# Two rows per partition, one 128-wide turn, and a last product formed transposed: three edits to the expert stage of a fused attention, soft-MoE and MLP kernel

## The chip, the cores and the metric

The kernel runs on one core of a Trainium2 chip. The time is that of one execution on the device, in microseconds (us). It was run three times: 636.4, 634.4 and 634.56 us, median 634.56 us. A fourth execution was recorded by the profiler; its own time is 633.09 us, of which the instructions span 631.3 us.

## What is computed

Three layers follow each other, on 4608 tokens of width 512:

```python
# 1 attention through 32 packed vectors, 8 batches x 8 heads, 576 rows each
p_packed = softmax(scale * p @ k.T) @ v
x = softmax(scale * q @ p_packed.T) @ p_packed      # rearranged to (4608, 512)
# 2 soft mixture of 8 experts, 4 slots each: 32 slots in all
logits = x @ phi                                    # (4608, 32)
slot_input = softmax(logits, over tokens).T @ x     # (32, 512)
for e in range(8):                                  # w1: 512x1024, w2: 1024x512
    slot_out[e] = relu(slot_input[e] @ w1[e]) @ w2[e]
y = softmax(logits, over slots) @ slot_out          # combine weights (4608, 32)
# 3 an MLP with h * tanh(softplus(h)), w_in: 512x2048, w_out: 2048x512, both float64 in memory
h = y @ w_in ; out = mish(h) @ w_out
```

The kernel never forms `y`: it multiplies the 32 rows of `slot_out` with `w_in` once (32x2048) and applies the combine weights to that product.

## The kernel before

The work is in three stages. The attention (up to about 162 us of the span) goes batch by batch. The expert stage (162 to about 217 us) reads the weights of the eight experts, 4 MB each, and forms `slot_out`. The MLP (to the end) goes through 18 blocks of 256 tokens and four groups of 512 hidden features; its products use fp32r operands in a high and a low part, and some of its blocks use a seven-product scheme (lines 1316 to 1367).

**Loads.** All weights come on the queue of SyncE (SP). The list `jobs` fixes their order: first and second weights of experts 0 to 5 in turn, with pieces of `w_in` between, then the first weights of experts 6 and 7, the second weights of 6 and 7, then `w_out`. Each job is a chunk of 512 KB. `plan` gives each job a place in large buffers (AW, AC, AY and others); `pump` issues the next job when the former user of its place is done. A first weight's chunk has 128 rows of 4 KB, one per partition (line 146). A second weight's chunk has 256 rows of 2 KB: partition p holds rows p and p+128 of the chunk, in two pieces (line 156). The very last chunk (expert 7, number 3) is read as two loads of half the size (line 154).

**One expert.** `ex_h(e)` multiplies the 32 slot inputs with `w1[e]` (line 989) and copies the hidden row block to SBUF (line 996). `ex_x(e)` picks the expert's four slots with the selection matrix `idm` and, with a VectorE transpose and a relu, leaves `h1T`: hidden features on partitions, 32 slots wide, eight blocks (lines 1004 to 1009). `ex_o(e)` multiplies each block with its rows of `w2[e]` (line 1016): `h1T` is the stationary operand of 32 columns, the weights are the moving one of 512 columns, and four blocks run side by side in four column strips of TensorE, each adding into its strip of the PSUM tile `so`. Rows of `so` other than the expert's four stay unchanged, since `idm` is zero there.

**Combine weights.** `combine(c)`, for batches 4c to 4c+3, is a generator of three parts: the softmax over slots, its normalisation, and the split in a high part `Hm`, `Hr` (fp32r) and a low part `Lm`, `Lr` (lines 1056, 1057). `combine_t(L, b)` turns one batch with TensorE, so that the tile CS holds high, low, high, low in strips of 32 partitions: 4 strips times 5 column blocks, 20 fp32 matmuls with 32-column weights (line 1068), then two copies to CS (line 1074).

**The end of the stage.** After `ex_o(7)`, VectorE copies the left half of `so` to SBUF (line 1419) and ScalarE the right half (line 1420); TensorE transposes the four quarters while summing the four strips with `ids` (line 1425); VectorE copies the result to SOT (line 1429). SOT times `w_in` (`emit_mp`, line 1141) opens the MLP; its second products are those of line 1327. `fill` is a filler matmul that nobody reads. The conversions of `w_out` (`cvt`) stand between on ScalarE and VectorE.

Each engine runs its instructions in the order in which they are written; a manual schedule fixes that order. In the profile one fp32 matmul counts as two weight loads and two passes, an fp32r one as one of each.

Of the kernel before, what the change touches and what calls it, by code (L numbers as in the profile page):

```python
# [19 lines left out]
def kernel(  # L20
# [24 lines left out]
    FT1 = F1 // 128  # L45
# [102 lines left out]

    def job_w2(e, c):
        def emit(t):  # L150
            if (e, c) == (E - 1, 3):
                for f in range(2):
                    r = 256 * c + 128 * f
                    nc.sync.dma_start(out=t[:, DM * f:DM * f + DM], in_=w2[e, r:r + 128, :])
                return
            nc.sync.dma_start(
                out=t[:, 0:2 * DM].rearrange("p (f n) -> p f n", f=2),
                in_=w2[e, 256 * c:256 * c + 256, :].rearrange("(f p) n -> p f n", p=128),
            )
        return emit  # L160

# [84 lines left out]
    ident = const.tile([128, 128], F32, name="ident")  # L246
# [10 lines left out]
    ids = const.tile([128, 32], F32, name="ids")  # L257
# [11 lines left out]
    si_acc = one.tile([128, HQ * D], F32, name="si_acc")  # L269
    st = {b: {} for b in range(B)}  # L270

    held = []

    def cv_z(nm, i, fold=True):

        if nm == "wi":
            name, dst = (nm, i // 4, i % 4), win[i // 2][:, 512 * (i % 2):512 * (i % 2) + 512]
        else:
            name = (nm, i)
            if 4 <= i < 8:  # L280
                if i % 2 == 0:
                    held.append(ring_a.tile([128, 18 * D], F32, tag=f"ring{i // 2 - 2}", name="held"))
                dst = held[i // 2 - 2][:, 512 * (i % 2):512 * (i % 2) + 512]
            else:
                dst = t2.tile([128, 512], F32, name="w64", tag="w64", bufs=4)
        tv = take(*name)[:, 0:1024].bitcast(I32).rearrange("p (n z) -> p n z", z=2)
        if fold:
            nc.scalar.activation(out=dst, in_=tv[:, :, 1].bitcast(F32), func=AF.Prelu, scale=2.0 ** -112, alpha=-(2.0 ** 32))
        else:
            nc.scalar.activation(out=dst, in_=tv[:, :, 1].bitcast(F32), func=AF.Copy, scale=2.0 ** -112)  # L290
        return nm, i, name, dst, dst.bitcast(I32), tv, fold
# [535 lines left out]
    x, y = B - 2, B - 1  # L827
# [143 lines left out]
    ex = {}  # L971
# [26 lines left out]

    def ex_x(e):

        h1 = ex[e][0].rearrange("p (k c j) -> p k c j", c=4, j=32)
        xp = ps_x.tile([128, FT1, M], F32, name="xp", tag="x")
        for c in range(4):
            nc.tensor.matmul(
                xp[32 * c:32 * c + 32], lhsT=idm[:, M * e:M * e + M], rhs=h1[:, :, c], start=True, stop=True,
            )
        h1T = two.tile([128, FT1, M], F32, name="h1T", tag="h1T")
        nc.vector.transpose(out=h1T.rearrange("p k m -> p (k m)"), in_=xp.rearrange("p k m -> p (k m)"))
        nc.vector.tensor_scalar_max(out=h1T, in0=h1T, scalar1=0.0)
        ex[e][1] = h1T  # L1010

    def ex_o(e, n=FT1, w=0, lo=0):
        h1T = ex[e][1]
        for ft in range(lo, n):
            g = ft % 4
            nc.tensor.matmul(
                so[32 * g:32 * g + 32], lhsT=h1T[:, ft], rhs=take("w2", e, ft // 2)[:, (ft % 2) * DM:(ft % 2 + 1) * DM],
                start=(e == 0 and ft < 4), stop=(e == E - 1 and ft >= n - 4),
            )
            if ft % 2:  # L1020
                done("w2", e, ft // 2)
                if ft < n - 1:
                    warm(w)

    def combine(c):

        if c:
            Lm, Hm = (two.tile([128, 512], F32, name=x, tag=x, bufs=1) for x in ("Lm", "Hm"))
        else:
            Lm, Hm = (t2.tile([128, 512], F32, name=x, tag="w64", bufs=4) for x in ("Lm", "Hm"))  # L1030
        Lm, Hm = (x.rearrange("p (b i m) -> p b i m", b=4, i=4) for x in (Lm, Hm.bitcast(F32R)))
        Lr = two.tile([64, 4, M], F32, name="Lr", tag="Lr")
        Hr = two.tile([64, 4, M], F32R, name="Hr", tag="Hr")
        both = ((128, 16, Lm.rearrange("p b i m -> p (b i) m"), Hm.rearrange("p b i m -> p (b i) m")), (64, 4, Lr, Hr))
        for n, k4, L, hi in both:
            lp = ps_x.tile([128, 4, 128], F32, name="clp", tag="x")
            for b in range(4):
                if n == 128:
                    nc.tensor.transpose(lp[:, b], LT[:, 4 * c + b, 0:128], ident)
                else:  # L1040
                    nc.tensor.transpose(lp[0:64, 0, M * b:M * b + M], LT[0:32, 4 * c + b, 128:192], ident[0:32, 0:32])
            xp = lp.rearrange("p b (i m) -> p (b i) m", m=M)[0:n, 0:k4]
            mx = two.tile([128, 16], F32, name="mxc", tag="mxc")
            nc.vector.reduce_max(out=mx[0:n, 0:k4], in_=xp, axis=AX.X)
            nc.vector.tensor_tensor(out=L, in0=xp, in1=mx[0:n, 0:k4, None].to_broadcast([n, k4, M]), op=ALU.subtract)
            nc.scalar.activation(out=L, in_=L, func=AF.Exp)
        yield
        for n, k4, L, hi in both:
            sm = two.tile([128, 16], F32, name="smc", tag="smc")[0:n, 0:k4]
            nc.vector.reduce_sum(out=sm, in_=L, axis=AX.X)  # L1050
            nc.vector.tensor_scalar_add(out=sm, in0=sm, scalar1=1e-9)
            nc.vector.reciprocal(out=sm, in_=sm)
            nc.gpsimd.tensor_tensor(out=L, in0=L, in1=sm[:, :, None].to_broadcast([n, k4, M]), op=ALU.mult)
        yield
        for n, k4, L, hi in both:
            nc.scalar.copy(out=hi, in_=L)
            nc.gpsimd.tensor_tensor(out=L, in0=L, in1=hi.bitcast(F32), op=ALU.subtract)
        Lc[c] = (Hm.bitcast(F32), Hr.bitcast(F32)), (Lm, Lr)
        yield

    def combine_t(L, b):

        cp = ps_h.tile([128, 2, 512], F32, name="cp", tag="hp")
        for i in range(NB):
            n = 128 if i < 4 else 64
            for g in range(4):
                src = L[g % 2][0][:, b % 4, i] if i < 4 else L[g % 2][1][:, b % 4]
                nc.tensor.matmul(
                    cp[32 * g:32 * g + 32, i // 4, (i % 4) * 128:(i % 4) * 128 + n], lhsT=src,
                    rhs=ident[0:n, 0:n] if i < 4 else ident[0:n, 0:n].rearrange("p (j r) -> p r j", j=2),  # L1070
                    start=True, stop=True,
                )
        for src, dst in ((cp[:, 0], CS[:, 512 * b:512 * b + 512]), (cp[:, 1, 0:64], CS[:, TB * 128 + 64 * b:TB * 128 + 64 * b + 64])):
            (nc.scalar.copy if b > 2 else nc.vector.tensor_copy)(out=dst, in_=src)

# [26 lines left out]
    ex_x(4)  # L1102
    next(cb)
    ex_o(4)
    next(cb)
    CS = arena.tile([128, NT], F32R, name="CS", tag="AC")
    combine_t(Lc[0], 0)
    combine_t(Lc[0], 1)
# [14 lines left out]
    ex_x(7)  # L1123
    ex_o(6)
    combine_t(Lc[1], 7)
    ex_o(7)
    late_w = {}
    so_sb = [two.tile([128, DM // 2], F32, name="so_sb", tag="h1") for _ in range(2)]
    SOT = t2.tile([128, 4, M], F32, name="SOT", bufs=1)
# [289 lines left out]
    nc.vector.tensor_copy(out=so_sb[0], in_=so[:, 0:256])  # L1419
    nc.scalar.copy(out=so_sb[1], in_=so[:, 256:512])  # L1420
    ba, bb = bank("x"), bank("x")
    fill(ba)
    cvt("z0 u0")
    for kt in range(4):
        nc.tensor.matmul(
            sot_ps[:, kt], lhsT=so_sb[kt // 2][:, 128 * (kt % 2):128 * (kt % 2) + 128], rhs=ids, start=True, stop=True,
        )
    fill(bb)
    nc.vector.tensor_copy(out=SOT, in_=sot_ps)
    ep.close()  # L1430
# [135 lines left out]
```

## Time and profile before

| | busy us | share of the span |
|---|---|---|
| TensorE matmuls (PE) | 603.5 | 96% |
| TensorE weight loads (PEld) | 522.3 | 83% |
| VectorE (DVE) | 499.5 | 79% |
| ScalarE (ACT) | 339.4 | 54% |
| GpSimd (POOL) | 47.3 | 7% |
| profiled execution | 633.09 whole | span 631.3 |

Busy TensorE time counts overlapping passes once and is no sign of its peak. The share of the 16 DMA engines is at nine tenths or more from about 110 to 221 us and low after that, so the expert stage and the MLP have different limits. HBM read 79.23 MB, written 9.44 MB. The clock row of the page shows nine tenths or more in all its 40 slices.

### The profile page before, as it was taken

What the parts mean: (1) busy time and instruction counts of PE and PEld (TensorE: products, weight loads), DVE (VectorE), ACT (ScalarE), POOL (GpSimd) and SP (SyncE); (2) the same over time, 40 slices, a digit from 0 to 9 for tenths busy, and PEclk for the clock granted to TensorE, in tenths of its full rate; (3) what the DMA queues carried; (4) which work ended last, traced back from release to release, by engine and by line L of the source; (5) the groups of instructions that cost most, each with busy time, mean ns of one, the idle gap of its engine ahead of it and who ended that gap; (6) DMA issues with size and microseconds to landing.
All of it is one profiled execution on the core that took longest, in us unless ns stands there. A gap on an engine that the chain in (4) does not pass through costs nothing.

```text
span 631.3 us, 14397 instructions
## 1 busy us (share of the span) xinstructions
PE 603.5 (96%) x5874; PEld 522.3 (83%) x5874; DVE 499.5 (79%) x1004; ACT 339.4 (54%) x684; POOL 47.3 (7%) x73
## 2 busy tenths in 40 slices
PE   7799999998998999999999999999999999999997
PEld 4577777786434468888989999999999999999997
DVE  4998888978464388988999887788778877887883
ACT  3354555546334486665556555555555555555551
POOL 5122222112030000000000000000000000000000
PEclk9999999999999999999999999999999999999999
DMA  8998963999999962002110110011011101110100
GB/s 274 329 323 293 330 210 128 404 412 407 394 410 413 413 243 67 2 0 68 35 35 0 35 35 12 24 34 34 2 34 34 34 2 34 34 34 2 34 34 35
DMA packets 42162, 89.61 MB, mean 142 GB/s; under 512 B 10736, under 2 KB 19056, under 8 KB 42096
## 3 DMA queue, kind: packets, MB, share of 16 engines
q1 hardware_dynamic: 41696, 88.36, 39.2%
q8 instruction: 46, 0.75, 0.5%
q10 hardware_dynamic: 144, 0.26, 0.1%
q14 instruction: 20, 0.16, 0.1%
q0 software_dynamic: 256, 0.07, 0.1%
HBM read 79.23 MB, written 9.44 MB: 140 GB/s over the span
## 4 chain that ended last, share of the span: by engine, by line
PE 65%; DVE 19%; DMA 8%; ACT 5%; issue 2%; SPq 1%; DVEq 0%; POOL 0%; ACTq 0%; POOLq 0%
PE o L1327 44%; PE so L1327 7%; DMA AW<-in_moe_w_dram 6%; PE h L1205 5%; DVE kT L338 4%; DVE S L1221 2%; DVE A L510 1%; DVE AY L1376 1%; DVE mx L509 1%; PE s L490 1%; DVE Sl L1240 1%; DVE sm L525 1%; DMA AW<-in_q_dram 1%; DVE nmx L386 1%; DMA AC<-in_k_dram 1%
## 5 line engine op out<-in xcount | busy, mean ns | idle before, releaser
L1327 PE MATMUL o<-W,gh 128*128 128x256 f32 (+1 forms) x648 | 119.2, 311 | 0.5 <-DVE AY L1376 0.5
L1327 PE MATMUL o<-T,Sh 128*128 128x256 f32 x708 | 114.8, 284 | 1.0 <-DVE AY L1376 0.9
L1236 ACT CAST gh<-AY 128x512 fp32r<-128x512 f32 x118 | 54.7, 511 | 113.5 <-PE o L1327 113.5
L1327 PEld LDWEIGHTS o<-W,gh 128*128 128x128 f32 x648 | 95.6, 188 | 7.9 <-issue 1.3
L1327 PEld LDWEIGHTS o<-T,Sh 128*128 128x128 f32 x708 | 97.0, 189 | 2.1 <-issue 0.6
L1210 ACT ACTIVATE AY<-h 128x512 f32<-128x512 f32 x126 | 74.0, 594 | 26.3 <-PE h L1205 25.0
L1239 DVE TENSOR_TENSOR gl<-AY,gh 128x512 fp32r<-128x512 f32 x118 | 60.4, 553 | 33.3 <-ACT gh L1236 33.3
L1240 DVE TENSOR_TENSOR Sl<-S,Sh 128x1024 fp32r<-128x1024 f32 x59 | 72.1, 1223 | 9.2 <-ACT Sh L1237 9.2
L1327 PE MATMUL o<-T,Sl 128*128 128x256 f32 x354 | 71.2, 282 | 0.0
L1327 PE MATMUL o<-W,gl 128*128 128x256 f32 (+1 forms) x324 | 70.0, 308 | 0.0
L1237 ACT CAST Sh<-S 128x1024 fp32r<-128x1024 f32 x59 | 61.9, 1049 | 6.8 <-DVE S L1221 6.8
L1205 PE MATMUL h<-CS,W 128*128 128x256 f32 x288 | 56.2, 284 | 0.0
L1327 PEld LDWEIGHTS o<-W,gl 128*128 128x128 f32 x324 | 52.1, 188 | 4.0
L1327 PEld LDWEIGHTS o<-T,Sl 128*128 128x128 f32 x354 | 54.8, 190 | 0.0
L1221 DVE TENSOR_TENSOR S<-AY 128x256 f32<-128x256 f32 x118 | 49.6, 420 | 6.0 <-ACT AY L1210 6.0
L1376 DVE TENSOR_TENSOR AY<-AY,o 128x256 f32<-128x256 f32 x115 | 45.1, 417 | 9.1 <-PE o L1327 5.3
L1205 PEld LDWEIGHTS h<-CS,W 128*128 128x128 f32 x288 | 44.1, 188 | 3.1 <-ACT s L1210 0.8
L1327 PE MATMUL so<-W,gh 128*128 128x256 f32 (+1 forms) x268 | 45.4, 292 | 0.0
L1327 PEld LDWEIGHTS so<-W,gh 128*128 128x128 f32 x268 | 37.3, 188 | 2.4 <-ACT W L1191 0.3
L376 PE MATMUL s<-kT,win 128*128 128x288 f32 x128 | 34.7, 414 | 4.7 <-ACT win L388 3.8
L1327 PE MATMUL o<-W,Sh 128*128 128x256 f32 x236 | 37.5, 281 | 0.0
L490 PE MATMUL s<-win,qT 128*128 128x128 f32 x256 | 32.1, 278 | 1.8 <-ACT win L356 1.8
(263 smaller groups left out, 988.9 us busy)
## 6 DMA issues: line engine op xcount, KB each, us to landing
AW<-in_moe_w_dram SPq DMA_DIRECT2D x45, 512.0 KB, 10.1
r_wo<-in_moe_w_out_dram SPq DMA_DIRECT2D x16, 512.0 KB, 8.9
out_dram<-AY SPq DMA_DIRECT2D x64, 128.0 KB, 2.1
r_wi<-in_moe_w_in_dram SPq DMA_DIRECT2D x13, 512.0 KB, 10.5
AW<-in_q_dram SPq DMA_DIRECT2D x11, 576.0 KB, 5.3
AW<-in_k_dram SPq DMA_DIRECT2D x9, 576.0 KB, 7.3
AW<-in_v_dram SPq DMA_DIRECT2D x40, 128.0 KB, 5.0
AC<-in_moe_w_dram SPq DMA_DIRECT2D x10, 512.0 KB, 10.0
```

The source lines that it names most:

```text
L338: nc.vector.transpose(out=T[:, dh, main].rearrange("p (i r a) -> p a i r" if nm == "k" else "p (i a r) -> p a i r", i=4, a=4,), in_=x[:, 0 ...
L376: nc.tensor.matmul(ps[:, n, 0:288], lhsT=pBD[b % 2][:, hq, dh], rhs=kT[:, dh, 288 * n:288 * n + 288], start=(dh == 0), stop=(dh == 1),)
L490: nc.tensor.matmul(ps[:, k - lo], lhsT=d["qT", hq][:, dh, 64 + 128 * i:192 + 128 * i], rhs=ppBD[b % 2][:, hq, dh], start=(dh == 0), stop=( ...
L1205: nc.tensor.matmul(hp[:, 256 * f:256 * f + 256], lhsT=MS[:, 128 * ft:128 * ft + 128], rhs=CS[:, 256 * n:256 * n + 256], start=True, stop=True,
L1210: nc.scalar.activation(out=s, in_=hp.rearrange("p (f n) -> p f n", f=2), func=AF.Mish)
L1221: nc.vector.tensor_tensor(out=S[:, k], in0=x, in1=y, op=op)
L1236: nc.scalar.copy(out=gh[:, f, t], in_=s[:, f, t])
L1237: nc.scalar.copy(out=Sh, in_=S)
L1239: nc.vector.tensor_tensor(out=gl[:, f, t], in0=s[:, f, t], in1=gh[:, f, t].bitcast(F32), op=ALU.subtract)
L1240: nc.vector.tensor_tensor(out=Sl, in0=S, in1=Sh.bitcast(F32), op=ALU.subtract)
L1327: nc.tensor.matmul(o, lhsT=lhsT, rhs=rhs, start=first, stop=stop)
L1376: add = lambda o, x, y: nc.vector.tensor_tensor(out=o, in0=x, in1=y, op=ALU.add)
```

## The change

1. *Second weights.* A chunk of `w2` is read so that partition p holds rows 2p and 2p+1, one piece of 4 KB. The last chunk is one load as well. `ex_x` picks its columns in the matching order, so its moving operand steps by two elements.
2. *Combine weights.* The split writes high, low, high, low side by side (each part twice, by a repeated read), in tiles `HL` and `HLr`. `combine_t` turns a column block with one fp32r matmul of 128 weight columns instead of four of 32; it reads an fp32r identity that GpSimd makes once. The buffers of 512 columns under the name `w64`, four of them, become two of 1024, shared by `HL` and converted `w_out` pairs. The third part of `combine(1)` moves behind the fourth `combine_t`.
3. *Expert 7.* `ex_o(7)` is dropped. `so` is complete after expert 6 and is copied and transposed into `sot_ps` while the last weights arrive; then 32 matmuls with the weights as stationary operand (128 columns) and `h1T` as the moving one (32 columns) add expert 7 there. One filler goes.

```diff
@@ job_w2
+                out=t[:, 0:2 * DM], in_=w2[e, 256 * c:256 * c + 256, :].rearrange("(p f) n -> p (f n)", f=2),
@@ ex_x
-        h1 = ex[e][0].rearrange("p (k c j) -> p k c j", c=4, j=32)
+        h1 = ex[e][0].rearrange("p (k c j f) -> p k f c j", c=4, j=32, f=2)
...
-                xp[32 * c:32 * c + 32], lhsT=idm[:, M * e:M * e + M], rhs=h1[:, :, c], start=True, stop=True,
+                xp[32 * c:32 * c + 32], lhsT=idm[:, M * e:M * e + M], rhs=h1[:, :, :, c], start=True, stop=True,
@@ combine, third part
-        for n, k4, L, hi in both:
-            nc.scalar.copy(out=hi, in_=L)
-            nc.gpsimd.tensor_tensor(out=L, in0=L, in1=hi.bitcast(F32), op=ALU.subtract)
+        T3 = [t2.tile([128, 1024], F32R, name="HL", tag="w64", bufs=2) for _ in range(2)]
+        T3.append(two.tile([64, 16 * M], F32R, name="HLr", bufs=1))
+        T3 = [t.rearrange("p (k g m) -> p k g m", g=4, m=M) for t in T3]
...
+            r = lambda x: x[:, :, None, :].to_broadcast([n, x.shape[1], 2, M])
+            nc.scalar.copy(out=t[:, :, 0:4:2], in_=r(L))
+            nc.gpsimd.tensor_tensor(out=t[:, :, 1:4:2], in0=r(L), in1=t[:, :, 0:4:2].bitcast(F32), op=ALU.subtract)
@@ combine_t
-            for g in range(4):
-                src = L[g % 2][0][:, b % 4, i] if i < 4 else L[g % 2][1][:, b % 4]
-                nc.tensor.matmul(
-                    cp[32 * g:32 * g + 32, i // 4, (i % 4) * 128:(i % 4) * 128 + n], lhsT=src,
...
+            n, src = (128, L[b % 4 // 2][:, 4 * (b % 2) + i]) if i < 4 else (64, L[2][:, b % 4])
+            nc.tensor.matmul(
+                cp[:, i // 4, (i % 4) * 128:(i % 4) * 128 + n], lhsT=src.rearrange("p g m -> p (g m)"),
+                rhs=ident_r if i < 4 else ident_r[0:n, 0:n].rearrange("p (j r) -> p r j", j=2),
@@ order of the expert stage
-    next(cb)
     CS = arena.tile([128, NT], F32R, name="CS", tag="AC")
...
     combine_t(Lc[0], 3)
+    next(cb)
     ex_x(5)
...
     combine_t(Lc[1], 7)
-    ex_o(7)
@@ end of the stage
-    fill(ba)
     cvt("z0 u0")
+    nc.tensor.matmul(sot_ps, lhsT=ident, rhs=idm[:, None, SPE:SPE + M].to_broadcast([128, 4, M]), start=True, stop=False)
     for kt in range(4):
         nc.tensor.matmul(
-            sot_ps[:, kt], lhsT=so_sb[kt // 2][:, 128 * (kt % 2):128 * (kt % 2) + 128], rhs=ids, start=True, stop=True,
+            sot_ps[:, kt], lhsT=so_sb[kt // 2][:, 128 * (kt % 2):128 * (kt % 2) + 128], rhs=ids, start=False, stop=False,
         )
+    for ft in range(FT1):
+        for kt in range(4):
+            r = DM * (ft % 2) + 128 * kt
+            nc.tensor.matmul(
+                sot_ps[:, kt], lhsT=take("w2", E - 1, ft // 2)[:, r:r + 128], rhs=ex[E - 1][1][:, ft], start=False,
+                stop=(ft == FT1 - 1 and kt == 3),
+            )
```

TensorE's order at the end of the expert stage, before: `xp` and `so` with x8 are experts 7 and 6, `cp` is the last batch's turn, and the second `so` row is expert 7; `o` is a filler and then SOT times `w_in`.

```order
L1004 MATMUL xp<-h_2838,idm 32x256 x4
L1016 MATMUL so<-AW,h1T 32x512 x8
L1068 MATMUL cp<-ident,Hm 32x128
L1068 MATMUL cp<-ident,Lm 32x128
...
L1016 MATMUL so<-AW,h1T 32x512 x8
L1417 MATMUL o_2936<-win_90,ident 128x256
L1425 MATMUL sot_ps<-ids,so_sb 128x32 x4
L1417 MATMUL o_2937<-win_90,ident 128x256
L1141 MATMUL o_2936<-win_90,SOT 32x256 x2
```

The same place after the change (lines are those of the new file); `sot_ps<-h1T,AW` is the new product of expert 7.

```order
L999 MATMUL xp<-h_2755,idm 32x256 x4
L1011 MATMUL so<-AW,h1T 32x512 x8
L1064 MATMUL cp<-ident_r,HL 128x128 x4
L1064 MATMUL cp<-ident_r,HLr 128x64
L1418 MATMUL sot_ps<-idm,ident 128x128
L1420 MATMUL sot_ps<-ids,so_sb 128x32 x4
L1426 MATMUL sot_ps<-h1T,AW 128x32 x32
L1412 MATMUL o_2816<-win_90,ident 128x256
L1136 MATMUL o_2815<-win_90,SOT 32x256 x2
```

The transposition of `so` now stands ahead of expert 7, and eight wide matmuls of it have become 32 narrow ones behind the transposition.

ScalarE's order in the middle of the stage, after the change: the casts of `HL` are the third part of `combine(1)`; before, one cast each of `Hm` and `Hr` stood ahead of the copy of `h` for expert 5, where nothing stands now.

```order
L1036 ACTIVATE Lm<-Lm 128x512
L1036 ACTIVATE Lr<-Lr 64x128
L991 COPY h_2646<-hp 128x1024
L283 ACTIVATE AY<-r_wi_2_2138 128x512
L283 ACTIVATE AY<-r_wi_3_2140 128x512
L1070 CAST CS<-cp 128x512
L1070 CAST CS<-cp 128x64
L1052 CAST HL<-Lm 128x16x32 x2
L1052 CAST HLr<-Lr 64x8x32
L991 COPY h_2718<-hp 128x1024
```

The split for batches 4 to 7 so comes after the turn of batch 3 and shortly before that of batch 4.

## Rows read from the trace of the kernel before

**Rows 1.** Windows: us, busy us (instructions) per engine, granted clock, DMA share, GB/s.

```profile
192.00:195.00 3.00, 1.59 (x44) 0.80 (x36) 2.72 (x7) 1.51 (x4) 0.00 (x0) 1.00 1.03 414
111.00:214.50 103.50, 95.28 (x1340) 57.78 (x1338) 67.02 (x158) 46.56 (x114) 13.97 (x17) 1.00 1.03 407
...
226.00:631.00 405.00, 399.49 (x3073) 382.58 (x3071) 332.90 (x641) 230.04 (x396) 0.85 (x1) 1.00 0.11 32
```

**Rows 2.** Chain that ended last, 185 to 260 us: start, us, what.

```profile
202.48 10.78 DMA AW<-in_moe_w_dram
...
213.30 2.29 PE so L1016 x8
...
217.71 0.61 PE o L1141 x8
...
225.63 1.16 PE so L1327 x4
...
236.44 0.47 PE h L1205 x4
```

**Rows 3.** Waits: PEld from 160 to 232 us, then PE from 225 us on.

```profile
PEld so L1016 <- DMA AW<-in_moe_w_dram: 4.6, 8, 1.4
...
PE o L1327 <- DVE AY L1376: 1.4, 4, 0.4
```

**Rows 4.** Windows while first weights, then second weights, of experts 6 and 7 land.

```profile
194.90:203.60 8.70, 8.48 (x126) 4.07 (x126) 2.00 (x6) 3.47 (x7) 0.00 (x0) 1.00 1.03 413
203.60:213.90 10.30, 9.51 (x126) 4.17 (x126) 3.34 (x9) 3.47 (x7) 0.00 (x0) 1.00 1.05 409
```

**Rows 5.** Groups by form, 162 to 226 us: count, busy us, mean ns.

```profile
L1068 PE MATMUL cp<-ident,Lm 128*32 128x128 f32 x128 | 10.6, 274 | 0.0
...
L1057 POOL TENSOR_TENSOR Lm<-Lm,Hm 128x512 f32<-128x512 f32 x2 | 2.6, 1280 | 0.4 <-ACT Hm L1056 0.4
...
L1425 PE MATMUL sot_ps<-ids,so_sb 128*128 128x32 f32 x8 | 1.1, 280 | 0.0
```

**Rows 6.** Timeline of ACT, then of PEld, around batch 4's turn.

```profile
193.09 0.70 ACT L1074 CAST CS<-cp 128x512 fp32r<-128x512 f32 x2 [0.28 <-PE cp L1068]
...
198.70 0.31 PEld L989 LDWEIGHTS hp<-AW,SIT 128*32 128x32 f32 x8 [0.55 <-DMA AW<-in_moe_w_dram]
```

**Rows 7.** Timeline of the end of the stage: start, us, instruction, wait before it.

```profile
207.65 0.12 PEld L1016 LDWEIGHTS so<-AW,h1T 128*32 128x32 f32 x2 [0.30 <-DMA AW<-in_moe_w_dram]
...
209.55 0.11 PEld L1016 LDWEIGHTS so<-AW,h1T 128*32 128x32 f32 x2 [1.35 <-DMA AW<-in_moe_w_dram]
...
210.00 0.60 PE L1016 MATMUL so<-AW,h1T 128*32 128x512 f32 x2
...
210.43 0.27 PE L1068 MATMUL cp<-ident,Hm 128*32 128x128 f32 x1
...
211.81 0.70 ACT L1074 CAST CS<-cp 128x512 fp32r<-128x512 f32 x2 [3.35 <-PE cp L1068]
212.03 0.14 PEld L1016 LDWEIGHTS so<-AW,h1T 128*32 128x32 f32 x4 [0.21 <-DMA AW<-in_moe_w_dram]
213.30 0.14 PEld L1016 LDWEIGHTS so<-AW,h1T 128*32 128x32 f32 x4 [1.13 <-DMA AW<-in_moe_w_dram]
...
214.54 0.14 PEld L1016 LDWEIGHTS so<-AW,h1T 128*32 128x32 f32 x2 [0.48 <-DMA AW<-in_moe_w_dram]
...
215.63 0.42 DVE L1419 COPY so_sb<-so 128x256 f32<-128x256 f32 x1 [6.31 <-PE so L1016]
...
216.14 0.37 ACT L1420 COPY so_sb<-so 128x256 f32<-128x256 f32 x1 [3.63 <-DVE so_sb L1419]
...
217.23 0.29 DVE L1429 COPY SOT<-sot_ps 128x128 f32<-128x128 f32 x1 [0.85 <-PE sot_ps L1425]
```

**Rows 8.** Chain, 120 to 162 us: fp32 passes with weights of 128 columns.

```profile
123.96 0.63 PE uq L658 x4
...
151.48 1.09 PE s L823 x8
```

More of the change, by code (lines that the diff above doesn't have):

```diff
@@ L150, in emit @@
         def emit(t):
[L151 to L155, printed above, removed]
             nc.sync.dma_start(
-                out=t[:, 0:2 * DM].rearrange("p (f n) -> p f n", f=2),
-                in_=w2[e, 256 * c:256 * c + 256, :].rearrange("(f p) n -> p f n", p=128),
+                out=t[:, 0:2 * DM], in_=w2[e, 256 * c:256 * c + 256, :].rearrange("(p f) n -> p (f n)", f=2),
             )
@@ L270 @@
     st = {b: {} for b in range(B)}
-    held = []
+    held, pair = [], [None]
     def cv_z(nm, i, fold=True):
@@ L279, in cv_z @@
             name = (nm, i)
-            if 4 <= i < 8:
-                if i % 2 == 0:
+            if i % 2 == 0:
+                if 4 <= i < 8:
                     held.append(ring_a.tile([128, 18 * D], F32, tag=f"ring{i // 2 - 2}", name="held"))
-                dst = held[i // 2 - 2][:, 512 * (i % 2):512 * (i % 2) + 512]
-            else:
-                dst = t2.tile([128, 512], F32, name="w64", tag="w64", bufs=4)
+                    pair[0] = held[-1]
+                else:
+                    pair[0] = t2.tile([128, 1024], F32, name="w64", tag="w64", bufs=2)
+            dst = pair[0][:, 512 * (i % 2):512 * (i % 2) + 512]
         tv = take(*name)[:, 0:1024].bitcast(I32).rearrange("p (n z) -> p n z", z=2)
@@ L1017, in ex_o @@
                 so[32 * g:32 * g + 32], lhsT=h1T[:, ft], rhs=take("w2", e, ft // 2)[:, (ft % 2) * DM:(ft % 2 + 1) * DM],
-                start=(e == 0 and ft < 4), stop=(e == E - 1 and ft >= n - 4),
+                start=(e == 0 and ft < 4), stop=(e == E - 2 and ft >= n - 4),
             )
@@ L1025, in combine @@
     def combine(c):
[L1027 to L1034, printed above, removed]
-        for n, k4, L, hi in both:
+        Lm = two.tile([128, 512], F32, name="Lm", tag="Lm", bufs=1).rearrange("p (k m) -> p k m", m=M)
+        Lr = two.tile([64, 4, M], F32, name="Lr", tag="Lr", bufs=1)
+        both = ((128, 16, Lm), (64, 4, Lr))
+        for n, k4, L in both:
             lp = ps_x.tile([128, 4, 128], F32, name="clp", tag="x")
@@ L1047, in combine @@
         yield
-        for n, k4, L, hi in both:
+        for n, k4, L in both:
             sm = two.tile([128, 16], F32, name="smc", tag="smc")[0:n, 0:k4]
@@ L1054, in combine @@
         yield
-        for n, k4, L, hi in both:
-            nc.scalar.copy(out=hi, in_=L)
-            nc.gpsimd.tensor_tensor(out=L, in0=L, in1=hi.bitcast(F32), op=ALU.subtract)
-        Lc[c] = (Hm.bitcast(F32), Hr.bitcast(F32)), (Lm, Lr)
+        T3 = [t2.tile([128, 1024], F32R, name="HL", tag="w64", bufs=2) for _ in range(2)]
+        T3.append(two.tile([64, 16 * M], F32R, name="HLr", bufs=1))
+        T3 = [t.rearrange("p (k g m) -> p k g m", g=4, m=M) for t in T3]
+        Lc[c] = T3
+        parts3 = [(128, Lm[:, 0:8]), (128, Lm[:, 8:16]), (64, Lr)]
+        for (n, L), t in zip(parts3, T3):
+            r = lambda x: x[:, :, None, :].to_broadcast([n, x.shape[1], 2, M])
+            nc.scalar.copy(out=t[:, :, 0:4:2], in_=r(L))
+            nc.gpsimd.tensor_tensor(out=t[:, :, 1:4:2], in0=r(L), in1=t[:, :, 0:4:2].bitcast(F32), op=ALU.subtract)
         yield
+    ident_r = t2.tile([128, 128], F32R, name="ident_r", bufs=1)
+    nc.gpsimd.tensor_copy(out=ident_r, in_=ident)
     def combine_t(L, b):
@@ L1064, in combine_t @@
         for i in range(NB):
-            n = 128 if i < 4 else 64
-            for g in range(4):
-                src = L[g % 2][0][:, b % 4, i] if i < 4 else L[g % 2][1][:, b % 4]
-                nc.tensor.matmul(
-                    cp[32 * g:32 * g + 32, i // 4, (i % 4) * 128:(i % 4) * 128 + n], lhsT=src,
-                    rhs=ident[0:n, 0:n] if i < 4 else ident[0:n, 0:n].rearrange("p (j r) -> p r j", j=2),
-                    start=True, stop=True,
-                )
+            n, src = (128, L[b % 4 // 2][:, 4 * (b % 2) + i]) if i < 4 else (64, L[2][:, b % 4])
+            nc.tensor.matmul(
+                cp[:, i // 4, (i % 4) * 128:(i % 4) * 128 + n], lhsT=src.rearrange("p g m -> p (g m)"),
+                rhs=ident_r if i < 4 else ident_r[0:n, 0:n].rearrange("p (j r) -> p r j", j=2),
+                start=True, stop=True,
+            )
         for src, dst in ((cp[:, 0], CS[:, 512 * b:512 * b + 512]), (cp[:, 1, 0:64], CS[:, TB * 128 + 64 * b:TB * 128 + 64 * b + 64])):
@@ L1421 @@
     ba, bb = bank("x"), bank("x")
-    fill(ba)
     cvt("z0 u0")
+    nc.tensor.matmul(sot_ps, lhsT=ident, rhs=idm[:, None, SPE:SPE + M].to_broadcast([128, 4, M]), start=True, stop=False)
     for kt in range(4):
         nc.tensor.matmul(
-            sot_ps[:, kt], lhsT=so_sb[kt // 2][:, 128 * (kt % 2):128 * (kt % 2) + 128], rhs=ids, start=True, stop=True,
+            sot_ps[:, kt], lhsT=so_sb[kt // 2][:, 128 * (kt % 2):128 * (kt % 2) + 128], rhs=ids, start=False, stop=False,
         )
+    for ft in range(FT1):
[4 more added lines that the diff above has]
+                stop=(ft == FT1 - 1 and kt == 3),
+            )
+        if ft % 2:
+            done("w2", E - 1, ft // 2)
     fill(bb)
```

## The prediction

> **What bounds the kernel now.** I read the windows by stage first. From 111 to 214.5 us the DMA engines are at a share of 1.03 and move 407 GB/s; from 226 us on that share is 0.11 and TensorE is busy 399 of 405 us [rows 1]. So the expert stage lasts as long as its weights take to arrive, and the MLP as long as TensorE takes. The chain of waits says the same at the seam: it runs over transfers until 213.3 us, then over the last expert's product, the transposition and SOT times `w_in` (217.71 us), and meets the MLP's second products at 225.63 us, after which it stays on TensorE [rows 2]. The waits show TensorE stopped eight times for second weights, 4.6 us in all, while from 225 us on it loses only 1.4 us to another engine [rows 3]. Two things follow. TensorE work that is removed inside the expert stage buys nothing as long as TensorE is waiting for a chunk anyway. And what delays SOT is not caught up later: nothing between SOT and 225.63 us waits for a transfer that is late, and the MLP has no slack.
>
> So the change is worth what it does to two moments: when the weights have landed, and how long after that SOT is ready. The timeline of the end [rows 7] gives the latter: the last half chunk is there at 214.54, the copy to SOT starts at 217.23, 2.69 us later.
>
> **Second weights, one piece of 4 KB.** The nearest comparison is in the trace: while first weights (4 KB pieces) land the rate is 413 GB/s, while second weights (2 KB pieces) land it is 409 [rows 4]. Up to expert 6 the second weights are 7 x 2.1 MB = 14.7 MB: 35.9 us at 409, 35.6 at 413, so 0.35 us gained. The end below starts when expert 6's last chunk is there (209.55). That chunk came 1.90 us after its predecessor (207.65), where later ones are 1.27 us apart (212.03 to 213.30) [rows 7]; if it comes regularly, another 0.6 us is gained. Bounds: 0 (no difference in rate) and 1.0. I take 0.5. The stepping read in `ex_x` is not in the trace; by the row of the product of SOT, eight passes of 256 columns in 0.61 us [rows 2], it lies between nothing and twice that. It runs beside transfers that keep going: a chunk is 10.78 us on its way [rows 2] while one lands every 1.27, so some eight are queued. I cost it at nothing; without that cover it would be 0.6 us for each expert whose product frees a buffer.
>
> **Combine weights.** The low-part half of the turns alone is 128 passes with 10.6 us of TensorE [rows 5]; that all falls to a quarter of the instructions or less. It stands between transfers, so I cost the saving at 0. The price is on other engines: per `combine` one more subtraction of 1.28 us on GpSimd [rows 5] and one more cast. For batches 4 to 7 the split now waits for batch 3's turn: ScalarE's copies of it began at 193.09 and took 0.70 [rows 6], then a cast (0.65, a little less than those two copies) and 1.28 us per subtraction give the first `HL` at 195.7, the second at 197.0 and the remainder by 198.0. Batch 4's turn, and expert 6's first product queued behind it on TensorE, may wait until 198.0; but that product then waits for its own chunk until 198.70 anyway [rows 6]. Cost 0; without that cover, up to 0.5 us.
>
> An fp32r turn with 128 columns is not in the trace. Below: an fp32r matmul with 128 weight columns and 256 moving ones goes every 0.47/4 = 0.12 us [rows 2]. Above: an fp32 one of the same weights is two passes at 0.11, 0.22 us (next part). The last batch's five so take 0.55 to 1.1 us, against 20 fp32 matmuls before. I take 0.55, by the row of the same type; this one counts, because it now stands on the path.
>
> **Expert 7 formed transposed.** This is the term that decides. Each of the 32 matmuls has fresh weights of 128 columns and is fp32, so it needs two weight loads and two passes: 64 of each. How fast such passes follow each other is in three places. Four passes of `uq` take 0.63 us: three steps and a last pass of about 0.28, so 0.117 at most and 0.11 if the last takes 0.30. Eight warm-up passes take 1.09, (1.09 - 0.28)/7 = 0.116 [rows 8]. The transposition of `so`, the same shape as the new matmuls (128 weight columns, 32 moving), has eight passes of 0.28 us in 1.1 us [rows 5]: (1.1 - 0.28)/7 = 0.117, with one wait inside. Moving only 32 columns does not make a step shorter than moving 128. I take 0.111: 64 x 0.111 = 7.1 us (7.0 to 7.4). A chunk thus costs 16 x 0.111 = 1.78 us of TensorE and arrives every 1.27 us: the end of the stage changes from waiting for DMA to waiting for weight loads.
>
> When can they start? By the times before:
>
> - 209.55 expert 6's last chunk is there; TensorE takes its next matmul at 210.43, the last sum of `so` is out at 210.00 + 0.60 = 210.60 [rows 7].
> - The last batch's turn, five loads, to 210.98; its results are out at about 211.15 (last start 210.87 + 0.28).
> - VectorE copies the left half of `so` at 210.65 to 211.07 (0.42). ScalarE stands before the right half with batch 7's two copies to CS, which are queued ahead of it: 211.2 to 211.9 (0.70), then 0.37 for the half [rows 7], so with the signal about 212.3.
> - The second half of the transposition: four loads, to 212.75.
> - 64 loads to 219.85; the last result 0.28 - 0.11 = 0.17 later, 220.0; the copy to SOT starts at 220.05.
>
> No chunk is late for this: the last one's passes begin at 212.75 + 48 x 0.111 = 218.1, and it landed at 214.54 [rows 7]. Against 217.23 this is 2.8 us later. The removed filler lay beside the copy of `so`, worth nothing.
>
> **Sum.** +2.8 for the end, -0.5 for the transfers before it: +2.3 us. On the profiled execution (633.09 us, the 631.3 of the span and 1.8 around it) that is 635.4. The three runs have a median 1.5 us above it, 634.56, so I predict 636.9 on their scale. What cannot be told from no change is about 0.3%, 1.9 us. The likeliest case's own range: 2.8 + 0.3 (slower loads) + 0.5 (the turn at its upper end) = +3.6 at worst, 2.8 - 1.0 - 0.6 = +1.2 at best (the last 0.6 if ScalarE's copies of batch 7 are out of the way): 635.8 to 638.2.
>
> The Trainium skill has a rule that would make the end cheaper. "TensorE: Matmul & The Clock Gate", section "Back-to-back issue gap", gives about 81 ns per matmul in a sustained stream of load and matmul pairs at 128 columns. By that figure 64 pairs would take 5.2 us, an estimate, and the sum would be +0.4 (the rival below that lets the passes keep up). The fp32 rows here stand against it, at 0.11 or more.
>
> **Rivals.**
>
> *The passes keep up.* If a step with 32 moving columns took 0.07 us, a chunk would cost no more than its 1.27 us. The passes still start where `so` lets them, at 212.75 - 0.5 = 212.25; they end at 216.7, and SOT's copy starts at 216.9, 0.3 us earlier than before: 634.3, not slower. It decides at 0.075 us per step, where the sum is 0; steps in between end at +0.4 (0.08) to +1.6 (0.10). For it: the weights of the next pass are loaded beside a running one, and the three rows are short runs of four or eight. Against it: all three agree on 0.11 or more, and one of them is the same shape.
>
> *The transfers gain more.* If pieces of 2 KB cost more than the two windows show, the whole end moves with expert 6's last chunk. From 2.8 us the sum falls below 0.3% at a gain of 0.9, and reaches +1.2 with 1.6: 635.8. For it: the irregular chunk at 209.55. Against it: 409 to 413 is 1%.
>
> "DMA: Bandwidth & Descriptors", section "Why small descriptors are slow", of the Trainium skill, names about 3 cycles of overhead per packet on beats of 32 bytes. For 2 KB against 4 KB that is 134 to 131 cycles, an estimate of 0.8 us on these bytes, half a microsecond more than I take; the two windows show less.
>
> *The clock falls.* TensorE does less between the chunks, and then streams few columns for 7 us. The granted clock is 1.00 even where TensorE was busy only 1.59 of 3 us [rows 1]. At 1.2 instead of 2.4 GHz the 64 loads would take 14.2 us and the time would be 644.
>
> *The end is slack.* If ScalarE and VectorE, not SOT, set 225.63 us, a late SOT costs less, say half, and the time is 635.7; they convert `w_out` there. Against it: SOT's copy at 217.23 is followed by its product at 217.71 on the chain, step by step.
>
> **How the numbers follow.** Forecast 0.63: of it 0.45 beyond 1.9 us, 0.18 within. Transfers gain more, or the end is slack: 0.17, all within 0.3%. The passes keep up, wholly or in part: 0.10, of it 0.08 within 0.3% and 0.02 faster, if the start comes earlier too. The clock falls: 0.05, slower. Anything else: 0.05, of it 0.03 faster, 0.02 slower. Together faster 0.05, within 0.3% 0.43, slower 0.52. The range reaches from steps of 0.08 us (+0.4, less 0.2 for a regular chunk) to the forecast's upper end: 634.8 to 638.2, and two tenths more above for a clock that falls for part of the way: 638.4.
>
> **What would show it.** Right: 64 weight loads in a row of some 7 us on `sot_ps`, starting before the last chunk lands and never waiting for a transfer after the first chunk or two; the copy to SOT 2 to 3 us later than 217.23; the first product of line 1327 later by as much; windows from 226 us on unchanged. Wrong: a wait for DMA on the last of these loads (then the passes keep up); an earlier landing of expert 6's last chunk by over a microsecond; a granted clock under 1.00; or the chain leaving TensorE between SOT and the MLP.

## The result, and the profile after

The changed kernel is slower: a median of 643.46 us (643.15 to 646.8, four runs) against 634.55 us (634.4 to 636.4, four runs), a ratio of 1.0146 with a 95% interval from 1.0107 to 1.0184. The forecast was 636.9 with a range up to 638.4, so the time lies outside it, 6.6 us above the forecast, and almost on the 644 of the rival in which the clock falls, which had a chance of 0.05. The profiled execution took 643.33 us, 641.5 of them span: 10.2 more than the span of the kernel before.

The windows of [rows 1], of the changed kernel (us, busy us and instructions of each engine, granted clock, DMA share, GB/s):

```profile
192.00:195.00 3.00, 0.74 (x12) 0.20 (x8) 2.97 (x7) 1.85 (x5) 1.87 (x2) 0.73 1.03 421
111.00:214.50 103.50, 94.08 (x1069) 56.77 (x1067) 70.84 (x160) 48.00 (x118) 18.56 (x20) 0.95 1.02 407
226.00:641.00 415.00, 409.67 (x3138) 387.14 (x3136) 340.77 (x655) 237.17 (x409) 0.85 (x1) 0.99 0.11 30
```

The transfers are as they were, and TensorE is as busy in the MLP. What is new stands in the third column from the right: the granted clock, 1.00 in the windows of [rows 1], is now under 1.00. Finer windows of the changed kernel show where it falls the second time and where it comes back:

```profile
211.00:212.60 1.60, 1.32 (x11) 1.17 (x11) 0.00 (x0) 0.98 (x3) 0.00 (x0) 1.00 1.03 420
212.60:213.80 1.20, 1.20 (x13) 1.20 (x13) 0.00 (x0) 0.00 (x0) 0.00 (x0) 1.00 1.03 423
213.80:214.10 0.30, 0.30 (x4) 0.30 (x3) 0.00 (x0) 0.00 (x0) 0.00 (x0) 0.59 1.00 410
214.10:225.40 11.30, 11.30 (x55) 11.30 (x54) 0.43 (x1) 1.35 (x2) 0.00 (x0) 0.50 1.01 406
225.40:230.80 5.40, 5.40 (x31) 2.32 (x30) 3.10 (x7) 1.97 (x5) 0.00 (x0) 0.50 0.07 30
230.80:231.20 0.40, 0.40 (x9) 0.06 (x1) 0.40 (x1) 0.40 (x1) 0.00 (x0) 0.85 0.00 0
231.20:234.00 2.80, 2.80 (x32) 1.15 (x28) 2.53 (x6) 2.77 (x6) 0.00 (x0) 1.00 0.23 34
```

The clock is at half (1.2 of 2.4 GHz) from 213.9 to 230.9 us, although TensorE is busy for the whole of that time; up to 225.4 us, where the last expert's passes end, the weight loads are busy throughout too. The "busy" column doesn't say how much the passes stream.

The end of the stage in the timeline, the counterpart of [rows 7]:

```profile
210.41 0.42 DVE L1414 COPY so_sb<-so 128x256 f32<-128x256 f32 x1
...
211.19 0.70 ACT L1070 CAST CS<-cp 128x512 fp32r<-128x512 f32 x2 [1.55 <-PE cp L1064]
...
211.78 0.39 ACT L1415 COPY so_sb<-so 128x256 f32<-128x256 f32 x1
212.22 0.52 PEld L1420 LDWEIGHTS sot_ps<-ids,so_sb 128*128 128x128 f32 x4 [0.39 <-ACT so_sb L1415]
...
212.69 12.79 PE L1426 MATMUL sot_ps<-h1T,AW 128*128 128x32 f32 x64
225.51 0.29 DVE L1433 COPY SOT<-sot_ps 128x128 f32<-128x128 f32 x1 [10.91 <-PE sot_ps L1426]
```

The passes start at 212.69 and never stop for a transfer, but last 12.8 us. The copy to SOT starts at 225.51 instead of 217.23: 8.28 us later. The chain [rows 2] shows what became of that:

```profile
212.85 12.62 PE sot_ps L1426 x64
225.47 1.01 PE o L1412 x2
226.49 1.87 PE o L1136 x16
...
235.77 0.70 PE so L1322 x3
```

The first of the MLP's second products starts at 235.77 instead of 225.63, 10.14 later, and the span is 10.2 longer. So between SOT and these products another 1.9 us were lost, where the clock was still at half, and nothing was made good afterwards. (The medians differ by 8.9, less than the spans, since the profiled execution of before lay 1.5 us under its median.)

The remaining rows answer to [rows 4] and [rows 5]: the windows while weights land, then groups by form from 162 to 236 us.

```profile
194.90:203.60 8.70, 8.70 (x39) 2.67 (x32) 1.93 (x2) 0.97 (x3) 1.64 (x2) 0.50 1.02 417
203.60:213.90 10.30, 9.48 (x84) 5.61 (x83) 4.94 (x11) 6.20 (x13) 0.00 (x0) 1.00 1.03 420
```

```profile
L1426 PE MATMUL sot_ps<-h1T,AW 128*128 128x32 f32 x64 | 12.8, 381 | 0.0
...
L1064 PE MATMUL cp<-ident_r,HL 128*128 128x128 f32 x32 | 6.0, 314 | 0.3 <-ACT h L991 0.3
L1053 POOL TENSOR_TENSOR HL<-Lm,HL 128x512 fp32r<-128x512 f32 x4 | 5.1, 1301 | 6.8 <-ACT HL L1052 6.8
```

Second weights now land at 420 GB/s, first ones at 417 (409 and 413 before). The combine turns are 32 passes with 6.0 us where the low half alone had 128 with 10.6. And the clock was at half for the whole first window, a first fall from about 193 to 203.6 us. In the waits of PEld from 160 to 232 us (us in total, times, longest), TensorE now waits for second weights twice, 0.6 us, where it was eight times and 4.6 [rows 3]:

```profile
PEld so L1011 <- DMA AW<-in_moe_w_dram: 0.6, 2, 0.3
```

In this execution it is TensorE that is late there, and not the weights. From 183 us to the copy of SOT the chain holds no transfer: it runs over TensorE, part of it at the low clock, and over ScalarE and VectorE. Three of its pieces, the first two at the low clock:

```profile
194.60 3.64 PE so L1011 x16
...
199.63 3.62 PE hp L984 x16
...
208.62 1.72 PE so L1011 x16
```

### The profile page after: what moved, and what is told of

Its sections match the earlier page's. It is cut to its first block, busy times and chain, and to the rows that moved or that the text cites. A ratio compares the mean times of both kernels' runs of the same rounds, so it can differ in the third digit from the quotient of the medians.

```text
span 641.5 us, 13942 instructions
## 1 busy us (share of the span) xinstructions
PE 614.0 (96%) x5642; PEld 532.8 (83%) x5642; DVE 503.3 (78%) x1004; ACT 340.0 (53%) x686; POOL 51.8 (8%) x76
## 4 chain that ended last, share of the span: by engine, by line
PE 72%; DVE 19%; ACT 5%; issue 2%; DMA 1%; DVEq 0%; SPq 0%; POOL 0%; ACTq 0%; POOLq 0%
PE o L1322 43%; PE so L1322 7%; PE h L1200 5%; DVE kT L333 5%; PE hp L984 3%; PE so L1011 2%; PE sot_ps L1426 2%; DVE S L1216 2%; DVE A L505 1%; DVE AY L1371 1%; PE s L371 1%; DVE mx L504 1%; PE s L485 1%; DVE Sl L1235 1%; DVE nmx L381 1%
```

## The experiments

All are compared with runs of the kernel before on their own chip, whose median was 633.9 to 634.0.

**The passes made wider.** The theory: the second fall comes from the 64 passes themselves, which bring 32 columns to each load of 128. Rivals: it comes from the work that the new combine turns took away before it, or from the loads, whatever the passes carry.

```diff
-                sot_ps[:, kt], lhsT=take("w2", E - 1, ft // 2)[:, r:r + 128], rhs=ex[E - 1][1][:, ft], start=False,
+                sot_w[:, kt], lhsT=take("w2", E - 1, ft // 2)[:, r:r + 128],
+                rhs=ex[E - 1][1][:, ft, None, :].to_broadcast([128, 4, M]), start=False,
```

> The changed kernel, but each of the last expert's 64 passes moves 128 columns instead of 32 (the activations four times over, into a PSUM tile four times as wide; the same 64 weight loads, the same start). Theory (narrow passes): the granted clock falls at 213.9 us because each load brings only 32 columns of work; with 128 it stays at 1.00 from 213 to 231 us, the 64 passes take 7 to 8 us instead of 12.7, SOT is copied near 220.5, the first product of the MLP's second matrix comes near 229, and the time is 637 (636 to 638.5). Rival (the earlier gap): the fall comes from the work that the new combine turns took out before 213 us; then the clock is 0.5 here too and the time stays at 643. Rival (weight loads): a stream of fp32 loads lets the clock fall whatever the columns; then also 643 or more.

Measured: 636.76 us, a ratio of 1.0052 (1.0029 to 1.0075). Its timeline, and the window of the passes:

```profile
213.38 7.39 PE L1427 MATMUL sot_ps<-h1T,AW 128*128 128x128 f32 x64
...
220.81 0.29 DVE L1435 COPY SOT<-sot_ps 128x128 f32<-128x128 f32 x1 [4.32 <-PE sot_ps L1427]
```

```profile
213.40:220.60 7.20, 7.20 (x66) 7.20 (x66) 0.43 (x1) 1.37 (x2) 0.00 (x0) 1.00 1.03 419
```

Four times the columns in 5.4 us less, with the same loads: the rival of the loads falls. That of the earlier gap falls only in part here. This kernel still has a first fall, but a shorter one (clock 0.69 from 195 to 198 us and 0.74 from 198 to 201). The runs with the old turns and with 64 columns, both below, settle it.

**Parts of the change.** First the last expert's product as before, everything else changed:

```diff
+    ex_o(7)
...
-    for ft in range(FT1):
-        for kt in range(4):
...
```

> Second weights in 4 KB pieces and the combine turns of 128 columns stay; the last expert's second product is formed as in the kernel before. Theory (narrow passes): the clock still falls near 193 us (less work between the chunks) but is back at 1.00 by 204 and stays there; the time is that of the kernel before less the transfers' gain: 633.9 (633.0 to 634.8). Rival (the earlier gap): the clock falls again near 214 us, and the time is 638 or more.

Measured: 632.37 us, ratio 0.9984 (0.9963 to 1.0005); the same kernel a second time, later, 632.22 us and 0.9983 (0.9965 to 1.0001). Its windows, then its timeline:

```profile
195.00:198.00 3.00, 3.00 (x16) 0.39 (x8) 1.79 (x2) 0.00 (x0) 1.50 (x2) 0.50 1.03 421
...
213.00:216.00 3.00, 3.00 (x20) 1.66 (x20) 1.33 (x4) 1.60 (x3) 0.00 (x0) 1.00 1.02 419
```

```profile
212.72 0.14 PEld L1011 LDWEIGHTS so<-AW,h1T 128*32 128x32 f32 x4 [0.68 <-DMA AW<-in_moe_w_dram]
...
215.43 0.29 DVE L1425 COPY SOT<-sot_ps 128x128 f32<-128x128 f32 x1 [0.85 <-PE sot_ps L1421]
```

The first fall is there, the second is not, and the loss is gone. Its time came 1.5 us below what was expected, too near to the interval's edge to be called a gain by itself. Treated as independent, the two series together give about 0.9983 (0.9970 to 0.9997).

Then the combine turns as before, the transposed product kept. The diff takes back the hunks of `cv_z`, `combine` and `combine_t` and the later place of the split.

> Second weights in 4 KB pieces and the last expert's transposed product stay; the combine turns are those of the kernel before (four of 32 columns for each new one). Theory (narrow passes): no fall near 193 us, but the clock falls near 214 all the same, the 64 passes take about 12.7 us, and the time is 643 (642 to 644). Rival (the earlier gap): the clock stays at 1.00 from 213 to 231 us, the passes take 7 us, and the time is 637.

Measured: 642.79 us, ratio 1.0137 (1.0107 to 1.0167). Its windows and the passes:

```profile
192.00:204.00 12.00, 10.39 (x178) 5.10 (x174) 5.03 (x12) 5.11 (x11) 0.00 (x0) 1.00 1.02 415
...
214.00:224.40 10.40, 10.40 (x53) 10.40 (x52) 0.43 (x1) 1.34 (x2) 0.00 (x0) 0.52 1.03 412
```

```profile
212.43 12.05 PE L1424 MATMUL sot_ps<-h1T,AW 128*128 128x32 f32 x64
```

No first fall, and the second all the same. The two falls are separate.

Last the layout of the second weights by itself; the diff takes back the combine hunks and the transposed product.

> Only the layout of the second weights is changed (two rows per partition in one piece of 4 KB, the very last chunk as one transfer); combine turns and last expert are those of the kernel before. It prices the term that was put at -0.5 us (bounds 0 to -1.0): the last chunk should land 0.4 to 0.9 us earlier than 214.54, but whole, so its second half is followed by four matmuls instead of two: the time is 634.0 (633.4 to 634.8), no fall of the clock anywhere from 190 to 231 us.

Measured: 633.69 us, ratio 0.9994 (0.9973 to 1.0015), 0.4 us with 1.3 either way. In the profiled execution the last chunk landed at 215.80, not earlier but later than 214.54:

```profile
215.80 1.05 PE L1010 MATMUL so<-AW,h1T 128*32 128x512 f32 x4 [0.19 <-DMA AW<-in_moe_w_dram]
```

In the kernel with the product as before, of the same layout, it was 212.72. With the old layout it moves as much: the last half, at 214.54 in the kernel before, landed at 216.70 in the run with 128 columns of the next experiment, which is the same kernel up to there. One execution differs from the next by more than this term, so a single trace can't price it, and the expectation on the landing was worth nothing. From the landing of the whole chunk to the copy of SOT it is 2.71 us in both (215.80 to 218.51; 212.72 to 215.43).

**The suspected cost by itself.** The kernel before, with 64 additional loads behind the transposition of `so`, once with passes of 32 and once of 128 columns:

```diff
-    fill(bb)
+    for i in range(32):
+        nc.tensor.matmul(bb[:, 0:32], lhsT=win[0][:, 128 * (i % 4):128 * (i % 4) + 128], rhs=ident[:, 0:32], start=True, stop=True)
```

> The kernel before, and between the transposition of so and the MLP 64 additional weight loads with passes of 32 columns each, into a PSUM bank that nothing reads; nothing of the change is in it. Theory (narrow passes by themselves): the clock falls 1 to 2 us after the first of them, they take 11.5 to 13 us, the clock stays at half for some us behind them, and the first product of line 1327 comes 9 to 11 us later than at 225.63: 643 to 645. Rival (something of the changed kernel, as its accumulation over four banks' parts or its weights fresh from a transfer): the clock stays at 1.00, the passes take 7.1 to 7.4 us, and the time is 640.5.

> The same 64 additional loads in the kernel before, with passes of 128 columns. Theory (narrow passes): the clock stays at 1.00, they take 7.2 to 7.5 us, and the time is that of the kernel before plus 6.5 to 7.5: 640.5 to 641.5. Rival (the loads): the clock falls here too and the time is 643 or more.

Measured: 646.1 us, ratio 1.0194 (1.0175 to 1.0214), with 32 columns; 641.33, ratio 1.0127 (1.0097 to 1.0156), with 128. The run with 32 columns, its passes and first product of line 1327, then its windows:

```profile
217.47 11.97 PE L1429 MATMUL o<-ident,win 128*128 128x32 f32 x64
...
238.59 1.32 PE L1327 MATMUL so<-W,gh 128*128 128x512 f32 x4
```

```profile
219.00:219.50 0.50, 0.50 (x7) 0.50 (x6) 0.00 (x0) 0.50 (x2) 0.00 (x0) 1.00 1.09 442
219.50:220.00 0.50, 0.50 (x5) 0.50 (x4) 0.00 (x0) 0.29 (x1) 0.00 (x0) 0.54 1.01 410
220.00:229.40 9.40, 9.40 (x49) 9.34 (x49) 0.00 (x0) 0.00 (x0) 0.00 (x0) 0.50 0.80 317
```

And with 128 columns:

```profile
219.19 7.39 PE L1429 MATMUL o<-ident,win 128*128 128x128 f32 x64
```

```profile
219.20:226.50 7.30, 7.30 (x66) 7.19 (x65) 0.90 (x2) 1.90 (x4) 0.00 (x0) 1.00 1.03 407
```

Nothing of the change is needed: the narrow passes make the clock fall 2 us after the first of them; the wide ones, with the same number of loads and four times the columns, don't, and are done 4.6 us sooner. The time with 32 columns came 1 us above what was expected; 12.96 us of delay at line 1327, against 9 to 11.

**Half as narrow.** 64 columns for each pass in the changed kernel; in the first experiment's diff the 4 becomes a 2.

> The changed kernel with 64 columns for each of the 64 passes (the activations twice over). Theory (narrow passes): what counts is how much the passes stream, so 64 lies between: either the clock holds (passes 7.1 to 7.4 us, 637) or it falls later than 1.2 us after the first pass (passes 8 to 12 us, 638 to 642). Rival (the wider opening matmul of the 128-column run kept the clock up, not the passes): the clock falls 1.2 us after the first pass as in the changed kernel, or 1.7 at most, the passes take 12 us or more and the time is 642.5 or more.

Measured: 636.26 us, ratio 1.0040 (1.0023 to 1.0056).

```profile
213.83 7.34 PE L1427 MATMUL sot_ps<-h1T,AW 128*128 128x64 f32 x64
```

```profile
213.80:221.00 7.20, 7.20 (x66) 7.20 (x66) 0.43 (x1) 1.36 (x2) 0.00 (x0) 1.00 1.03 417
```

The clock holds here too, and this kernel has the first fall in full (clock 0.50 from 195 to 204 us): the earlier gap doesn't bring the second fall about. The opening matmul is half as wide as in the first experiment but still twice that of the changed kernel (256 columns against 128), so this run alone doesn't clear it; the pair above, which has no such matmul, does.

**Only the last chunk transposed.**

```diff
+    ex_o(7, FT1 - 2)
...
-    for ft in range(FT1):
+    for ft in range(FT1 - 2, FT1):
```

> The changed kernel, but only the last of the last expert's four chunks is formed transposed (16 loads with passes of 32 columns); the first three are summed in so as before, and so is turned while the last chunk lands. Theory (narrow passes let the clock fall, but not at once: in the changed kernel the clock fell 1.2 us after the first of them): 16 passes at 0.111 take 1.8 us, the clock is at most low for a moment, and the copy to SOT starts some 0.5 us earlier than in the kernel that keeps the last expert's product whole (215.4): 214.9, time 632 (631 to 634). Rival (any such passes cost the clock at once): the clock is 0.5 from 213 to some 220 us, the seam's products take twice as long, and the time is 635 or more.

Measured: 635.2 us, ratio 1.0018 (0.9998 to 1.0037). The median is the rival's time, though by neither account, and the interval reaches down to no change. The passes, then the windows behind the first of them:

```profile
216.44 1.09 PE L1421 MATMUL sot_ps<-ids,so_sb 128*128 128x32 f32 x8
217.37 1.95 PE L1427 MATMUL sot_ps<-h1T,AW 128*128 128x32 f32 x16
```

```profile
218.40:219.10 0.70, 0.70 (x9) 0.70 (x8) 0.00 (x0) 0.48 (x1) 0.00 (x0) 1.00 1.06 433
219.10:222.40 3.30, 3.30 (x21) 1.39 (x21) 1.93 (x5) 1.38 (x3) 0.00 (x0) 0.54 1.02 412
```

The 16 passes took 1.95 us, nearly the 1.8 expected; the clock fell at 219.3, 2.0 us after the first of them, as the last one ended, and it was the MLP's first products that ran at half. The gain of 0.5 us was not there either: the passes came straight behind the turn of `so`, which had taken the chunk's place on the path. In this execution the clock stayed at 1.00 from 192 to 204 us, though the combine turns are the new ones.

**A faster version?** The kernel with the product as before, with the very last chunk in two transfers, and the same with nine matmuls of 128 columns where TensorE waits before expert 5's second product.

```diff
+            if (e, c) == (E - 1, 3):
+                src = w2[e, 256 * c:256 * c + 256, :].rearrange("(p f) n -> p f n", f=2)
+                for f in range(2):
+                    nc.sync.dma_start(out=t[:, DM * f:DM * f + DM], in_=src[:, f])
+                return
...
     ex_x(5)
+    for _ in range(9):
+        nc.tensor.matmul(wps[:, 0:128], lhsT=ident, rhs=ident, start=True, stop=True)
     ex_o(5)
```

> The kernel with 4 KB pieces and the new combine turns but the last expert's product as before, a second time, beside other runs of the kernel before: its first ratio was 0.9984 with an interval from 0.9963 to 1.0005. If the transfers' gain of 0.5 us and nothing else is there, 633.4 against 633.9 (0.9992); if the first ratio was no chance, 0.998.

> The same kernel, and the very last chunk arrives in two transfers again (one row of each pair each), so that two matmuls instead of four are left when the last half lands. In the kernel before the copy to SOT starts 2.69 us after the last half landed at 214.54; with the last chunk whole it started 2.71 us after its landing. So the half must save its wait by landing at the same time: gain 0 to 0.3 us, time 632.4 to 633.9.

> The kernel with two halves, and nine matmuls of 128 columns, whose result nobody reads, where TensorE waits some 2.2 us for the transposed activations of expert 5. Theory (little streaming lets the clock fall, and near 193 us it falls beside transfers that are late anyway): the clock stays at 1.00 from 192 to 204 us, and the time is that of the kernel with two halves within 0.3%. Rival (the low clock there delays the buffers and so the transfers): the last chunk lands earlier and the time is 1 us or more shorter.

The first of these three is the second series told of above (632.22 us). Measured for the others: 632.95 us, 0.9993 (0.9976 to 1.0010), in two halves; 632.71 us, 0.9985 (0.9966 to 1.0003), with the filling. The windows of the gap with the filling, and without it in the second run of the kernel with the product as before:

```profile
192.00:195.00 3.00, 2.94 (x30) 2.32 (x34) 2.96 (x7) 2.10 (x6) 1.64 (x2) 1.00 1.03 423
195.00:198.00 3.00, 3.00 (x27) 1.11 (x19) 2.08 (x2) 0.39 (x1) 1.79 (x2) 1.00 1.03 421
```

```profile
192.00:195.00 3.00, 0.74 (x12) 0.22 (x11) 2.96 (x7) 2.03 (x6) 1.70 (x2) 0.72 1.03 422
195.00:198.00 3.00, 3.00 (x16) 0.38 (x8) 2.01 (x2) 0.00 (x0) 1.72 (x2) 0.50 1.02 416
```

In the run with two halves, from which the filled one differs by nothing else, the fall was shorter: 0.79 from 195 to 198 us and 0.64 from 198 to 201. One trace of each could mislead, but the other executions bear it out: the mean granted clock of a whole execution has a median of 0.997 with the filling and of 0.992 without, over 12 each. So the filling holds the clock in most executions, and no difference in time can be measured from it (the intervals of the two lie almost on each other): the first fall costs nothing that shows. Two executions of the kernel with the product as before say the same: both took 631.32 us, at mean clocks of 0.989 and 0.996. No gain from either addition can be shown. The version with 4 KB pieces, the new turns and the old product has the lowest times found, some 0.17% below the kernel before; the filled one can't be told from it.

## Why the prediction was wrong, point by point

- **What bounds the kernel: right for the MLP, only in part for the end of the expert stage.** Nothing between SOT and the MLP's products takes up a delay; 8.28 us at SOT became 10.14 at the first product and 10.2 in the span. The rival of a slack end is out. But in the changed kernel's execution TensorE hardly waited for weights any more (0.6 us against 4.6), and the chain ran over TensorE's own work.
- **Second weights, -0.5: neither contradicted nor shown.** By itself the layout gave 0.4 us with 1.3 either way; the window of second weights went from 409 to 420 GB/s, that of first weights, whose layout is the same, from 413 to 417 [rows 4]. (The prediction sets an estimate of 0.8 beside its 0.5 and calls the difference half a microsecond; it is 0.3.)
- **Combine weights, 0: not contradicted.** With the old product the new turns came to 0.9984, the old ones to 0.9994, each with 0.2% either way. The subtraction of 1.28 us on GpSimd came as 1.30, and the last batch's five turns stand on the chain with 0.83 us, within 0.55 to 1.1 (the row that the 0.55 was taken from gives 5 x 0.12 = 0.6). Not foreseen: with less of this work TensorE's clock fell near 193 us. In the changed kernel that low clock lay on the chain, but no time measured shows a cost of it.
- **Start of the passes: right, in part by luck.** 212.25 by the sum (212.75 less 0.5), 212.69 in the trace. ScalarE's copies came as written (CS from 211.19, the half of `so` done by 212.2). What let them start was something else: the sum has expert 6's last chunk release the last sum of `so` by 210.60, and in the trace that product ran from 208.62 to 210.34 behind TensorE's own work, without waiting for its chunk.
- **Passes at 0.111 us: right at full clock.** (7.39 - 0.28)/63 = 0.113 us with 128 or, by (7.34 - 0.28)/63, 0.112 with 64 columns. The figure of 81 ns in the Trainium skill ("TensorE: Matmul & The Clock Gate", section "Back-to-back issue gap") is not reached by these fp32 loads in any run here.
- **64 x 0.111 = 7.1 us: the step that failed.** It took the full clock for granted. After the first eleven passes the clock was at half, and a step took 0.213 us instead of 0.112 (52 steps from 213.98 to 225.07 us): 12.6 us for all on the chain, 5.5 too much. Then 1.9 us more were lost until the clock came back. With 0.4 for the later start these make 7.8 us over the sum's +2.3, of the span's +10.2.
- **The rival "The clock falls" was what happened,** and a clock under 1.00 was one of the prediction's own signs of being wrong. It was given 0.05. Its time of 644 came out partly by luck: it has 14.2 us for the loads, which took 12.6 since the first ran at full clock, and leaves out the 1.9 us lost behind them. The reason given for so little was one row: a clock of 1.00 where TensorE was busy for only 1.59 of 3 us [rows 1]. That row is of gaps between passes that stream 64 to 512 columns; it says nothing on passes that keep TensorE "busy" and stream little. The three places from which 0.111 was read [rows 5, 8] are runs of four or eight passes, over within 1.1 us, so they could not show a fall that comes 1.2 us (changed kernel) or 2 us (passes alone) after the first.

In the times, the cost of the clock is the difference between the changed kernel and the one with passes of 128 columns: 1.0146 to 1.0052, 0.94% or 6.0 us, with 2.8 either way by the two intervals (6.7 us by the run with 64 columns). The trace's 5.5 and 1.9 us, 7.4 together, lie within. What remains, 1.0052 against 0.9984 for the product as before, 0.7% or 4.3 us with 2.0 either way (3.6 by 64 columns), is the transposed product itself (predicted: +2.8 us and up to 0.8 for slower loads and turns; the wider opening matmul of that run, 1.13 us against 0.49, is in it as well).

## What to carry to other kernels

A duration read from a handful of instructions holds for the clock that stood there: before a long run of narrow passes is priced, work out what it costs at either level, and what is queued behind it until the clock returns. Busy share doesn't tell whether the clock will hold, and where a fall is suspected, widening the moving operand at the same number of loads is a cheap test (here it made the work shorter, not longer). Before a product is formed so that its result comes out transposed, compare its loads with the transfers they stand beside: here a chunk of 512 KB needed 1.8 us of loads at full clock and landed every 1.27, and even at full clock the kernel was 0.4 to 0.5% slower than the kernel before.

## What was not expected of the hardware

- The clock fell after 1.20 of 1.20 us in which TensorE was busy, and stayed at half through another 11.30 of 11.30. The Trainium skill ("TensorE: Matmul & The Clock Gate", section "HAM oscillation — how this bites in real kernels") names gaps in which TensorE waits as what lets it fall. The first fall has such a gap beside it, a wait of 2.26 us for `h1T` ahead of 194.60, and where that gap was filled the clock held. For the second the measurement decides against it as the only way.
- It stayed at half for 5.4 us after the last narrow pass (225.5 to 230.9 us), with TensorE busy throughout; with the old turns for 3.6 us, and in the kernel before with the 64 passes added for 3.8.
- What stays open: in one execution with the new turns (the last chunk alone transposed) the clock did not fall near 193 us, though TensorE was busy for only 0.75 of 3 us there as well, with a wait of 2.25 us for `h1T`. In the other unfilled ones it fell to half, for about 10 us in four and about 3 us in two. No run tells why.
